# Two placements in an attention and SwiGLU kernel: PSUM tile and copy engine of batch 1's first transposes, and the gap of the second-softmax value product

## The chip, the cores and the metric

One core of a Trainium2 chip runs the whole program. The metric is device time in microseconds (us), lower is better; a time is the median of several executions. Before: 369.15 us (368.29 to 369.44, three runs), and 369.29 us with a fourth run (369.80), the value that the changed kernel is compared with.

Engines: PE multiplies matrices, VectorE (DVE) and ScalarE (ACT) do elementwise work, GpSimd (POOL) issues the casting and gathering transfers and a few masks, SP issues plain and transposing transfers. PEld in the profile is PE's weight load, which overlaps its matmuls here: PE is busy for 350.1 us and PEld for 175.2 us of a span of 366.2.

## The reference, cut to what matters

```python
# q, k, v: (8 batches, 8 heads, 576 positions, 64); 8 global positions
mask = |i - j| <= 32  or  i is global  or  j is global
attn = softmax(where(mask, q @ k.T / 8, -1e9))
x    = (attn @ v) laid out as (8 * 576 tokens, 512)
out  = (silu(x @ w_gate) * (x @ w_val)) @ w_out        # 512 -> 1536 -> 512
```

## The kernel before

The feed-forward part runs in nine chunks of 512 tokens, each of twelve gate units and four output units. After each unit comes a gap into which pieces of the attention of later batches are put by hand, in the order in which they are written. A piece that wasn't ready held up what follows it in the profile of before: PE sat idle 2.52 us ahead of the first transposes of batch 1, and the next gate, which needs nothing of them, started behind them at 35.27 us.

The score matmuls of this kernel read q and k with the head dimension on partitions (64 of them: `ps_s<-qT,kT 64*128 64x64` in the profile). Batches 0 to 2 transpose on PE (step T). The global keys' and queries' scores come from gathered rows that POOL masks into a tile kqm, transposed on PE (step GT). The "second softmax" is that of the global queries over all keys: its weights p are transposed into p2t (step P2T; by PE up to batch 3, by a DMA transpose on SP for batches 4 to 7) and multiplied with v (step AV2, line 462). The result becomes gvt on DVE, which each later value product (step AV, line 546) reads first.

```python
psc = tile_pool(bufs=1, space=PSUM)   # score pair, tag "sc"
pm  = tile_pool(bufs=1, space=PSUM)   # tile m
pf  = tile_pool(bufs=4, space=PSUM)   # gates and outputs

def step_T(hp):                       # one head pair of batch 1 or 2
    pool, tag = (pm, "m") if (hp in (0, 2) if b == 1 else hp == 3) else (psc, "sc")
    pair = pool.tile([P, 2, 1024], BF16, tag=tag, name="ps_t")
    # ... 12 transposes of k, 12 of q
    nc.scalar.copy(out=kT[...], in_=pss[0])
    (nc.scalar.copy if hp % 2 else nc.vector.tensor_copy)(out=qTs[b][...], in_=pss[1])

def gate(fc):
    if t0 == 0 and fc == 2:
        pair = pm.tile([P, 2, CH], FP32, tag="m", name="pgv")   # gate 2 borrows tile m
    # ... 4 matmuls to pg, 4 to pv; then ACT: tanh; DVE: gv = (th + 1) * pg; h = gv * pv

def loads_b():                        # POOL, in this order
    load_qk_part(1, loaded[1], 0); load_qk_part(1, loaded[1], 1)
    load_wgv(2)
    g1 = gather(1)
    load_v(1, range(0, 3))
    kqms[1] = gather_mask(*g1)
    load_v(1, range(3, 5))
    # ... output weights

# casts of k and q of batch b to bf16 in DRAM (POOL), o = 16 * (b - 1):
    if b > 4: cast_at[b] = o - 32 + 8
```

The softmax here doesn't subtract the row's maximum and nothing guards it: scores larger than these inputs give would overflow.

Of the kernel before, what the change touches and what calls it, by code (L numbers as in the profile page):

```python
# [26 lines left out]
def kernel(  # L27
# [11 lines left out]
    nc = tc.nc  # L39
# [32 lines left out]
    psc = ctx.enter_context(tc.tile_pool(name="psc", bufs=1, space=bass.MemoryType.PSUM))  # L72
    pm = ctx.enter_context(tc.tile_pool(name="pm", bufs=1, space=bass.MemoryType.PSUM))
# [264 lines left out]
    def attention(b):  # L338
# [24 lines left out]
        def step_T(hp):  # L363
            if hp == 0:
                qTs[b] = bp.tile([P, HP, S], BF16, tag="qT", name="qT")
            pool, tag = (pm, "m") if (hp in (0, 2) if b == 1 else hp == 3) else (psc, "sc")
            pair = pool.tile([P, 2, 1024], BF16, tag=tag, name="ps_t")
            pss = []
            for n, name in enumerate(("k", "q")):
                ps = pair[:, n, 0:S].rearrange("p (j i) -> p j i", j=LJ)  # L370
                pss.append(ps)
                src = loaded[b][name]
                for j in range(LJ):
                    for par in range(2):
                        nc.tensor.transpose(  # L375
                            out=ps[64 * par : 64 * par + 64, j, :],
                            in_=src[:, 2 * hp + par, D * j : D * (j + 1)],
                            identity=ident[0:LP, 0:LP],
                        )
            nc.scalar.copy(  # L380
                out=kT[:, hp, WIN : WIN + S].rearrange("p (i j) -> p i j", j=LJ),
                in_=pss[0].rearrange("p j i -> p i j"),
            )
            (nc.scalar.copy if hp % 2 else nc.vector.tensor_copy)(
                out=qTs[b][:, hp, :].rearrange("p (i j) -> p i j", j=LJ),
                in_=pss[1].rearrange("p j i -> p i j"),
            )
# [256 lines left out]
        L = lambda f, *a: (lambda: f(*a))  # L644
# [31 lines left out]
        if b < XQ:  # L676
            return [
                [L(step_T, 0)], [L(step_T, 1)],
                *([[L(step_T, 2)], [L(step_GT), L(step_T, 3), vb]] if b == 1 else
                  [[L(step_GT), L(step_T, 2)], [L(step_T, 3), vb]]),  # L680
            ] + mid + end
# [2 lines left out]
            [L(step_S2), L(step_SG)],  # L684
            [L(step_S, 0), L(step_P2T)],
            [],
            [L(step_S, 1)],
            [L(step_S, 2), L(step_AV2)],
            [L(step_S, 3), L(step_AV, 0), L(step_X, 0)],
            [L(step_AV, 1), L(step_X, 1)],  # L690
            [L(step_S, 4), L(step_AV, 2), L(step_X, 2)],
# [91 lines left out]


    head, xa2, xa3, s4, av8, x8 = attention(0)
    for f in head:
        f()
# [32 lines left out]
    for b, o in ((1, 2), (2, 15)):  # L820
        for i, g in enumerate(attention(b)):
            gaps[o + i] = gaps.get(o + i, []) + g
    for b in range(XQ, B):
        steps = attention(b)
        o = 16 * (b - 1)
        for i, g in enumerate(steps):
            slot = o + 1 + (16 * i) // len(steps)
            gaps[slot] = gaps.get(slot, []) + g
        if b > XQ:
            tr_at[b] = o - 16 + 5  # L830
        if b > 4:
            cast_at[b] = o - 32 + 8
        v_at[b] = o - 16 + 2
        g_at[b] = o - 16 + 6
        m_at[b] = o - 16 + 13
# [43 lines left out]
```

## Time and profile before

| before | value | read as |
|---|---|---|
| median | 369.15 us | 368.29 to 369.44 |
| profiled execution | 367.98 us, span 366.2 us | the profile of one execution |
| PE busy | 350.1 us, 96% | the bound |
| DVE, ACT, POOL busy | 64%, 42%, 27% | off the path except where PE waits for them |
| granted TensorE clock | 1.000 in the profiled execution | 9 in all 40 slices of the row PEclk |

A line of the waits view reads: who waited, for whom, then total us, number of waits and the longest. A line of the timeline reads: start, duration, engine, line, operation, out<-in, shape, count, and in brackets the idle time before it and what ended it.

### The profile page before, as it was taken

How to read it: one execution, taken by the hardware profiler on the slowest of the kernel's cores; microseconds unless marked ns; L12 is line 12 of the kernel's file. 1: busy time of each engine (PE TensorE's matmuls, PEld its weight loads, DVE VectorE, ACT ScalarE, POOL GpSimd, SP SyncE). 2: the span in 40 equal slices, each digit the busy share in tenths (PEclk: the TensorE clock that was granted, in tenths of full speed). 3: DMA queues.
4: the chain of work that ended last, by engine and by line, in shares of the span. 5: the costliest groups of instructions: out<-in, count | busy, mean ns of one | idle time of the engine just before them, and what ended most of it. 6: DMA issues, size and time to landing. Idle time of an engine off the chain costs nothing.

```text
span 366.2 us, 7993 instructions
## 1 busy us (share of the span) xinstructions
PE 350.1 (96%) x3290; PEld 175.2 (48%) x3290; DVE 235.3 (64%) x469; ACT 152.8 (42%) x237; POOL 97.5 (27%) x114
## 2 busy tenths in 40 slices
PE   2887999999999999999999999999999999999996
PEld 1564545554544454444444454444544454444444
DVE  6665787268944885588548854886488728824850
ACT  4734573467323552355225532552354323323322
POOL 7925455934444001450246013100000000000000
PEclk9999999999999999999999999999999999999999
DMA  7999999999999926999999999941340131011002
GB/s 103 142 209 204 120 188 200 167 214 138 140 160 199 191 55 111 138 141 150 147 141 139 157 131 145 175 69 54 107 100 2 43 113 27 0 57 60 0 9 109
DMA packets 141638, 43.52 MB, mean 119 GB/s; under 512 B 126369, under 2 KB 135841, under 8 KB 141601
## 3 DMA queue, kind: packets, MB, share of 16 engines
q0 software_dynamic: 93824, 19.40, 64.4%
q1 hardware_dynamic: 47776, 23.60, 31.2%
q8 instruction: 26, 0.43, 0.5%
q14 instruction: 12, 0.09, 0.1%
HBM read 38.28 MB, written 15.34 MB: 146 GB/s over the span
## 4 chain that ended last, share of the span: by engine, by line
PE 80%; DMA 10%; POOL 4%; DVE 3%; ACT 2%; issue 1%; POOLq 0%; DVEq 0%
PE po L772 25%; PE pg L711 23%; PE pv L711 22%; DMA kg<-in_k_dram,gofs 4%; DMA wg_sb<-in_moe_w_gate_dram 3%; PE ps_av L546 3%; PE ps_s L493 2%; DMA vb<-va 2%; PE ps_av L555 2%; ACT pe L501 1%; POOL va L102 1%; DMA va<-in_v_dram 1%; DVE pt L507 1%; DVE gvt L469 1%; PE po L759 1%; PE ps_t L375 1%
## 5 line engine op out<-in xcount | busy, mean ns | idle before, releaser
L711 PE MATMUL pg<-xT,wg_sb 128*128 128x512 bf16 x420 | 108.3, 380 | 0.0
L711 PE MATMUL pv<-xT,wv_sb 128*128 128x512 bf16 x420 | 107.8, 379 | 0.0
L744 DVE SCALAR_TENSOR_TENSOR gv<-th,pg 128x512 bf16<-128x512 bf16 x107 | 73.3, 685 | 39.7 <-ACT th L742 39.0
L742 ACT ACTIVATE th<-pg 128x512 bf16<-128x512 f32 x107 | 63.9, 598 | 80.5 <-PE pg L711 76.7
L772 PE MATMUL po<-wo_sb,h 128*128 128x512 bf16 x420 | 94.5, 379 | 0.0
L748 DVE TENSOR_TENSOR h<-gv,pv 128x512 bf16<-128x512 bf16 x107 | 73.6, 688 | 11.5 <-PE pg L711 0.5
L711 PEld LDWEIGHTS <-wv_sb 128*128 128x128 bf16 x424 | 41.5, 98 | 50.0
L772 PEld LDWEIGHTS <-h 128*128 128x128 bf16 x420 | 39.9, 98 | 46.3
L102 POOL DMA_DIRECT2D va<-in_v_dram x40 | 35.2, 989 | 96.9 <-PE ps_av L555 73.5
L711 PEld LDWEIGHTS <-wg_sb 128*128 128x128 bf16 x424 | 37.0, 98 | 40.9 <-issue 1.7
L777 ACT ACTIVATE osb<-po 128x512 f32<-128x512 f32 x35 | 20.9, 597 | 81.7 <-PE po L772 79.7
L501 ACT ACTIVATE pe<-ps_s 128x1024 bf16<-128x1024 f32 (+1 forms) x40 | 37.5, 938 | 17.3 <-PE ps_s L493 16.6
L507 DVE TENSOR_TENSOR pt<-pe,band 128x1024 bf16<-128x1024 bf16 (+1 forms) x40 | 25.4, 636 | 20.3 <-ACT pe L501 20.3
L522 DVE TENSOR_REDUCE den<-ps_av 128x8 f32<-128x16 f32 (+1 forms) x40 | 6.7, 168 | 35.9 <-PE ps_av L555 33.6
L528 DVE TENSOR_TENSOR xa<-ps_av,den 128x512 bf16<-128x512 f32 (+1 forms) x40 | 25.5, 638 | 1.6 <-DMA xT<-xa 0.2
L546 PE MATMUL ps_av<-gvt,pg 128*64 128x264 bf16 x128 | 18.1, 295 | 1.0 <-DVE gvt L477 1.0
L493 PEld LDWEIGHTS <-kT 64*128 64x128 bf16 x576 | 11.3, 98 | 16.0 <-issue 15.0
L555 PE MATMUL ps_av<-va,pt 128*64 128x66 bf16 x256 | 18.0, 198 | 0.0
L555 PEld LDWEIGHTS <-pt 128*64 128x64 bf16 x512 | 17.6, 114 | 0.8 <-DMA vb<-va 0.7
L555 PE MATMUL ps_av<-vb,pt 128*64 128x66 bf16 x256 | 17.7, 198 | 0.3 <-DMA vb<-va 0.2
L493 PE MATMUL ps_s<-qT,kT 64*128 64x64 bf16 x576 | 16.2, 196 | 1.1 <-ACT pe L501 1.1
L109 POOL DMA_DIRECT2D qf<-in_q_dram x5 | 14.0, 2806 | 0.0
(122 smaller groups left out, 220.7 us busy)
## 6 DMA issues: line engine op xcount, KB each, us to landing
out_dram<-osb SPq DMA_DIRECT2D x35, 256.0 KB, 2.1
vb<-va SPq DMA_DIRECT2D x14, 264.0 KB, 5.6
va<-in_v_dram POOLq DMA_DIRECT2D x24, 128.0 KB
kf<-in_k_dram POOLq DMA_DIRECT2D x5, 576.0 KB
qf<-in_q_dram POOLq DMA_DIRECT2D x5, 576.0 KB
k_bf<-in_k_dram POOLq DMA_DIRECT2D x6, 288.0 KB
q_bf<-in_q_dram POOLq DMA_DIRECT2D x6, 288.0 KB
va<-in_v_dram POOLq DMA_DIRECT2D x16, 96.0 KB
```

What stands on the lines that cost most here:

```text
L102: nc.gpsimd.dma_start(out=va[lo:hi, u, :, 0:D], in_=vs[t0 + lo : t0 + hi])
L493: nc.tensor.matmul(out=ps[:, par, 64 * slot : 64 * slot + 64], lhsT=kT[r : r + 64, hp, 64 * t : 64 * t + P], rhs=qTs[b][r : r + 64, hp, 64 ...
L501: nc.scalar.activation(out=pe, in_=ps[:, :, 0 : 64 * ns].rearrange("p r (s c) -> p r s c", c=64), func=AF.Exp, scale=SCALE,)
L507: mult = lambda: nc.vector.tensor_tensor(out=pt.rearrange("p r s c -> p (r s) c"), in0=pe.rearrange("p r s c -> p (r s) c"), in1=bc(band, ...
L528: nc.vector.tensor_tensor(out=xa.rearrange("p (g h) d -> p g h d", g=g), in0=bc(ps, pst + [[1, D]]), in1=bc(den, [[4, g], [1, 4], [0, D]]) ...
L546: nc.tensor.matmul(out=ps[64 * e : 64 * e + 64, hg], lhsT=st["pg"][:, P * tp + 64 * e : P * tp + 64 * e + 64], rhs=st["gv"].rearrange("p h ...
L555: nc.tensor.matmul(out=ps[64 * e : 64 * e + 64, hg, hl, :], lhsT=pt[:, hl % 2, 4 * (hl // 2) + 2 * (tp % 2) + e, :], rhs=(va if e == 0 els ...
L711: nc.tensor.matmul(out=ps[:, 0:n], lhsT=w[:, cc, P * fc : P * (fc + 1)], rhs=xT[:, cc, t0 : t0 + n], start=(cc == 0), stop=(cc == NCC - 1),)
L742: nc.scalar.activation(out=th[:, 0:n], in_=pg[:, 0:n], func=AF.Tanh, scale=0.5)
L744: nc.vector.scalar_tensor_tensor(out=gv[:, 0:n], in0=th[:, 0:n], scalar=1.0, in1=pg[:, 0:n], op0=ALU.add, op1=ALU.mult,)
L748: nc.vector.tensor_tensor(out=st["h"][:, fc, 0:n], in0=gv[:, 0:n], in1=pv[:, 0:n], op=ALU.mult)
L772: nc.tensor.matmul(out=po, lhsT=st["h"][:, fc, P * ts : P * (ts + 1)], rhs=wo_sb[:, fc, :], start=(fc == 0), stop=(fc == NFC - 1),)
```

## The change

The intent: gate 2 fills tile m, and the first transposes of batch 1, next on PE, want the same tile; they wait until DVE has read it, 2.52 us in the profile of before. In the score pair they need not wait. That pair is needed again by the next head pair, so both copies go to ScalarE. Second, the value product of the second softmax is put behind the second score group in place of the third, so that gvt is ready when the first value product asks for it.

```diff
-            pool, tag = (pm, "m") if (hp in (0, 2) if b == 1 else hp == 3) else (psc, "sc")
+            pool, tag = (pm, "m") if hp == (2 if b == 1 else 3) else (psc, "sc")
@@
-            (nc.scalar.copy if hp % 2 else nc.vector.tensor_copy)(
+            (nc.scalar.copy if hp % 2 or (b == 1 and hp == 0) else nc.vector.tensor_copy)(
@@   steps of batches 3 to 7
-            [L(step_S, 1)],
-            [L(step_S, 2), L(step_AV2)],
+            [L(step_S, 1), L(step_AV2)],
+            [L(step_S, 2)],
```

"Part one" below is the first two edits, "part two" the third.

## The prediction

> **What bounds the kernel now.** I read the busy shares first, then the waits of PE, then the timeline around each wait that the change aims at, and last the landing times of the transfers that the moved work reads.
>
> ```profile
> span 366.2 us, 7993 instructions
> PE 350.1 (96%) x3290; PEld 175.2 (48%) x3290; DVE 235.3 (64%) x469; ACT 152.8 (42%) x237; POOL 97.5 (27%) x114
> ```
>
> PE is the bound: it is idle for 366.2 - 350.1 = 16.1 us in all, so only what shortens or lengthens PE's idle time, or adds PE work, can move the end. The change adds no PE instruction. The waits of PE are therefore the whole account:
>
> ```profile
> PE ps_t L355 <- DMA k_bf<-in_k_dram: 6.4, 2, 6.1
> PE ps_t L375 <- DVE h L748: 2.5, 1, 2.5
> ...
> PE ps_av L546 <- DVE gvt L477: 1.0, 5, 0.2
> ...
> PE ps_av L555 <- DMA vb<-va: 0.2, 1, 0.2
> ```
>
> The second line is what part one removes, the third is what part two removes: 2.5 + 1.0 = 3.5 us, 0.9% of the span, if nothing takes their place. Columns are total, times, longest. The last line, 0.2 us for the shifted values vb, looks like nothing; it matters below.
>
> [...] the first transposes of batch 1 sit idle 2.52 us for the gate values, and the next gate, which needs nothing of them, starts after them at 35.27 us. [...] the transposed second softmax p2t lands 9.8 us after issue while casts of k and q issued on POOL are under way, 2.7 us when none is. [...] the same p2t issue is recorded as 2.24 us, against 9.8 us to landing.
>
> **Part one: first transposes of batch 1.** Before, the transposes of head pair 0 use the PSUM tile m that gate 2 has just filled, and wait until DVE has read it.
>
> ```profile
> 34.64 0.45 PE L375 MATMUL ps_t<-ident,k_bf 96*64 96x96 bf16 x12 [2.52 <-DVE h L748]
> 34.89 0.45 PE L375 MATMUL ps_t<-ident,q_bf 96*64 96x96 bf16 x12
> 35.27 1.04 PE L711 MATMUL pg<-xT,wg_sb 128*128 128x512 bf16 x4
> ```
> ```profile
> 33.50 0.91 POOL L102 DMA_DIRECT2D va<-in_v_dram  x1 [0.61 <-DMA q_bf<-in_q_dram]
> ...
> 41.65 0.40 POOL L247 TENSOR_TENSOR kqm<-kg,mka 128x128 bf16<-128x128 f32 x1 [5.80 <-DMA kg<-in_k_dram,gofs]
> 42.01 0.39 POOL L247 TENSOR_TENSOR kqm<-qg,mka 128x128 bf16<-128x128 f32 x1
> ```
>
> In the score pair the k transposes can start at 32.05 us, where the first weight load already stood. They take 34.89 - 34.64 = 0.25 us. The q transposes then wait for q_bf: the last increment of its semaphore is at 33.22 us in the trace's records. They take 35.27 - 34.89 = 0.38, so gate 3 starts near 33.22 + 0.04 + 0.38 = 33.64, not 35.27: 1.6 us sooner. That is the local gain, the rest of the 2.5 is already lost to q_bf.
>
> It does not last. Three gates later PE transposes kqm. It came there at 42.29, so it will come at 42.29 - 1.6 = 40.7; but POOL makes kqm only when the gathered keys land (41.51 by the records), at 41.65 + 0.40 = 42.05 and 42.01 + 0.39 = 42.40. POOL and that gather do not wait for PE. The second kqm transpose was at 42.46 before and will be there again: the 1.6 us turns into a wait on POOL of about 1.6. If it slipped through, the vb transfer would catch it: it lands at 55.48 by the records, and the first product with vb starts at 55.52 already. The DMA that feeds it (keys, values, vb) hangs on no PE work here.
>
> Moving the q copy adds one ACT copy (0.65 us, as the odd head pairs show) and removes one DVE copy (0.76). The next transposes also use the score pair and need both copies done: the k copy ends near 33.4, the q copy runs from about 33.75 to 34.4, and the next transposes come at 33.64 + (37.37 - 35.27) = 35.7. No wait, 1.3 us to spare. Part one is worth **0.0 us**.
>
> **Part two: second-softmax product one gap sooner, batches 3 to 7.** The order of instructions shows that the 20 matmuls of L462 move from behind the third score group to behind the second, two gates sooner; their DVE multiplies follow. Removed: five waits of 0.2 us of the first value product on gvt, 1.0 us. Batch 5 before:
>
> ```profile
> 203.28 0.41 PE L493 MATMUL ps_s<-qT,kT 64*128 64x64 bf16 x16
> 203.62 1.04 PE L711 MATMUL pg<-xT,wg_sb 128*128 128x512 bf16 x4
> ...
> 207.18 0.41 PE L493 MATMUL ps_s<-qT,kT 64*128 64x64 bf16 x16
> 207.52 0.47 PE L462 MATMUL ps_av<-va,p2t 128*32 128x132 bf16 x20
> ...
> 210.35 0.30 PE L546 MATMUL ps_av<-gvt,pg 128*64 128x264 bf16 x2 [0.19 <-DVE gvt L477]
> ```
> ```profile
> 195.29 2.24 SPq L448 DMA_TRANSPOSE p2t<-p  x1
> ```
> ```profile
> DMA to landing us min/median/max: 9.8/9.8/9.8
> ```
>
> The product used to be asked for at 207.52; it will be asked for at 203.62, the end of the second score group. Its p2t is issued at 195.29 and lands 9.8 us later (the last line is the landing view of p2t in this stretch): 195.29 + 9.8 = 205.1. **Two gates of slack were hiding a late transfer.** New wait in batch 5: 205.08 + 0.04 - 203.62 = 1.5 us (0.04 as for vb above).
>
> The same for the others, with the landing from the semaphore records: batch 4, asked for at 166.06, landed 167.03: wait 1.0 us. Batch 6, asked at 241.19, landed 232.81 + 2.7 = 235.5: none. Batch 7, asked at 278.75, landed 270.38 + 3.4 = 273.8: none. Batch 3 transposes on PE, and its copy ends at 124.31, asked for at 128.49: none. Batches 4 and 5 are late because the casts of k and q for later batches are issued at 154.91 and 192.46, just ahead of their p2t; for 6 and 7 there is no cast left. These starts are all paced by PE, so a shift of PE by some tenths moves both sides and leaves the waits.
>
> Nothing else grows: m is free when the product comes (its last reader, the exponential of the global scores, ended long before), and the 1.07 us of DVE multiplies move to a gap followed by one without attention work.
>
> **Sum.** Part one 0.0; part two -1.0 + 1.0 + 1.5 = +1.5 us. After batch 5 PE has no wait left in which to win it back, and all later work is PE's. From the median 369.15 I take **370.4 us**: 0.2 below the full sum[...].
>
> **Rivals.** (A) Both waits vanish and nothing replaces them: 369.15 - 3.5 = 365.7. For it speaks the list of waits; against it the kqm multiply and vb, both within 0.3 us of binding already. (B) p2t lands in time in batches 4 and 5, as in 6 and 7: -1.0, so 368.1. For it: [...] I have one trace; against: two batches of two with casts are late, by 1.0 and 1.5, and landings would have to improve by about a tenth each. (C) Part one lives in part, where gather and vb land sooner than in this trace: at most 1.6 less, so 368.8 with the waits of part two. (D) The two copies on ACT delay the next transposes in the shared score pair: at most some tenths, in front of the same kqm wait, so it costs nothing at the end. I give my own account about 70%, B 13%, C 12%, A 5%.
>
> **Range and chances.** The runs of before spread 1.15 us. Rival B gives the low side, landings half a microsecond later each the high side: 368.5 to 371.9. A gain of 2% would be 7.4 us, twice what all touched waits hold; a loss of 2% would need p2t five times as late. Faster 0.01, same 0.98, slower 0.01.
>
> **What would show it.** In the profile after: no wait of L375 on h; a short one of the q transposes on q_bf; a wait of L393 on kqm of more than 1 us, and the second kqm transpose still near 42.5; no wait of L546 on gvt; two waits of L462 on the DMA of p2t of about 1.0 and 1.5 us, in batches 4 and 5 alone. Wrong would be: the kqm transposes more than half a microsecond sooner (the gather moved with PE), or L462 without waits (B).

0.0 for part one and -1.0 + 1.0 + 1.5 for part two came to +1.5 us, 370.65 on the median of 369.15. That the forecast lies some 0.2 us lower, at 370.4, was the author's guess.

## The result, and the profile after

The changed kernel took **367.88 us** (367.72 to 368.09, four runs) against 369.29 us: ratio 0.9965, 95% interval 0.9943 to 0.9987. That is 0.35% faster, "same" at the 2% mark, and below the predicted range of 368.5 to 371.9.

The page of the changed kernel, span and busy line:

```profile
span 366.2 us, 7940 instructions
PE 345.8 (94%) x3236; PEld 175.2 (48%) x3290; DVE 235.5 (64%) x468; ACT 153.2 (42%) x238; POOL 96.6 (26%) x114
```

PE seems less busy, but 54 of its 3290 matmul records are missing here (the weight loads are complete), so this share can't be compared. The span is the same as before to 0.1 us, although the medians differ by 1.4: the two profiled executions, 367.98 and 367.97 us, were equally fast. So the profiles side by side can't show the gain; the difference must lie in what executions of before mostly do and its first profile did not.

The longest waits of PE in the changed kernel, after the 6.9 us on k_bf at the start:

```profile
PE ps_av L462 <- DMA p2t<-p: 2.0, 2, 1.3
PE ps_av L555 <- DMA vb<-va: 1.5, 1, 1.5
PE ps_s L493 <- ACT pe L501: 1.1, 1, 1.1
PE ps_av L462 <- DMA va<-in_v_dram: 0.6, 2, 0.4
```

The 2.5 us on h and the 1.0 us on gvt are gone. In place of the latter are two waits on p2t, as predicted. The waits on vb and va belong to batch 0, whose work the change doesn't touch; there this execution lost about 2 us that the first profile of before had not lost. The timeline of the changed kernel:

```profile
34.11 0.45 PE L375 MATMUL ps_t<-ident,k_bf 96*64 96x96 bf16 x12
34.39 0.42 PE L375 MATMUL ps_t<-ident,q_bf 96*64 96x96 bf16 x12
34.74 1.04 PE L711 MATMUL pg<-xT,wg_sb 128*128 128x512 bf16 x4
...
41.76 0.28 PE L393 MATMUL ps_g<-ident,kqm 128*128 128x128 bf16 x2
...
164.61 0.41 PE L493 MATMUL ps_s<-qT,kT 64*128 64x64 bf16 x16
166.34 0.36 PE L462 MATMUL ps_av<-va,p2t 128*32 128x132 bf16 x12 [1.32 <-DMA p2t<-p]
...
203.31 0.41 PE L493 MATMUL ps_s<-qT,kT 64*128 64x64 bf16 x16
204.39 0.41 PE L462 MATMUL ps_av<-va,p2t 128*32 128x132 bf16 x16 [0.68 <-DMA p2t<-p]
```
```profile
41.03 0.39 POOL L247 TENSOR_TENSOR kqm<-qg,mka 128x128 bf16<-128x128 f32 x1
```

The two lines of L462 are cut by the end of the stretch asked for; the product has 20 matmuls. Three readings. The transposes start without a wait. kqm was ready at 41.03 + 0.39 = 41.42 us, not at 42.40 as in the first profile of before, and PE, late from batch 0, came after it: no wait there. And p2t was late in batches 4 and 5, by 1.32 and 0.68 us.

### The profile page after: what moved, and what is told of

The parts are those of the page before. It is cut to its first block, busy times and chain, and to the rows that moved or that the text cites. A ratio compares the mean times of both kernels' runs of the same rounds, so it can differ in the third digit from the quotient of the medians.

```text
span 366.2 us, 7940 instructions
## 1 busy us (share of the span) xinstructions
PE 345.8 (94%) x3236; PEld 175.2 (48%) x3290; DVE 235.5 (64%) x468; ACT 153.2 (42%) x238; POOL 96.6 (26%) x114
## 4 chain that ended last, share of the span: by engine, by line
PE 85%; DMA 9%; POOL 2%; issue 1%; ACT 1%; DVE 0%; POOLq 0%; DVEq 0%
PE po L772 25%; PE pg L711 24%; PE pv L711 22%; DMA p2t<-p 5%; PE ps_s L493 3%; PE ps_av L546 3%; DMA vb<-va 2%; PE ps_av L555 2%; DMA va<-in_v_dram 2%; PE ps_t L375 1%; POOL va L102 1%; PE ps_av L462 1%; PE ps_s L427 1%; PE po L759 1%; PE ps_x L604 1%
## 5 line engine op out<-in xcount | busy, mean ns | idle before, releaser
L711 PE MATMUL pg<-xT,wg_sb 128*128 128x512 bf16 x390 | 105.9, 380 | 1.9 <-issue 0.3
L772 PE MATMUL po<-wo_sb,h 128*128 128x512 bf16 x404 | 92.4, 379 | 0.6 <-issue 0.2
```

The lines of the kernel that those rows point to most:

```text
L711: nc.tensor.matmul(out=ps[:, 0:n], lhsT=w[:, cc, P * fc : P * (fc + 1)], rhs=xT[:, cc, t0 : t0 + n], start=(cc == 0), stop=(cc == NCC - 1),)
L772: nc.tensor.matmul(out=po, lhsT=st["h"][:, fc, P * ts : P * (ts + 1)], rhs=wo_sb[:, fc, :], start=(fc == 0), stop=(fc == NFC - 1),)
```

## The experiments

Sixteen runs were made, in four sets of four, each set on one chip with its own runs of before (e3, e4, e13 and e14 repeat earlier kernels). Each run also has the mean granted clock of each timed execution, and that turned out to be the key. Three theories went in. **H**: the first profile of before had an unusually early batch 0 on PE. **P**: p2t is in time in most executions. **C**, formed after the first set: the 2.5 us of PE idle is often followed by a stretch of half clock.

### e1 and e2: the parts alone; e3 and e4: both kernels profiled again

Edits: the first two hunks of the change (e1), the third (e2), none (e3, e4).

> Part one alone (transposes of head pair 0 of batch 1 in the score pair, both copies on ScalarE). The prediction on record: 0.0 us, the wait for the gate values turns into a wait of L393 on kqm. Theory H (head): in the profile of after, batch 0 ran about 2 us later on PE than in the profile of before, because its vb and va landed later, so that kqm and vb of batch 1 no longer bound and the whole 2.5 us was kept; if most executions have such a late head, part one alone gains 2.0 to 2.5 us. Theory P (the waits on p2t seen in the profile of after are short in other executions): part one gains under 0.5 us.

> Part two alone (second-softmax value product one gap sooner in batches 3 to 7). Prediction on record: loses 1.5 us; the profile of after showed waits on p2t of 2.0 us against 1.0 us saved, so theory H expects a loss of 0.7 to 1.5 us, with two waits of L462 on p2t in batches 4 and 5. Theory P expects a gain of 0.5 to 1.4 us.

> The kernel before once more, for a second profile of its head. Theory H: the first value product of batch 0 that needs vb starts later than the 23.65 us of the first profile (towards 25.5), the wait of L375 on h is still 2.5 us and there is no wait of L393 on kqm; span about 1.5 us longer than 366.2. If the head is as in the first profile, span about 366.2 and theory H falls.

> The changed kernel once more, for a second profile. Theory H: either a late head again (batch 0 waits 1 to 2 us on vb or va, no wait of L393 on kqm) or an early head with a wait of L393 on kqm; in both, waits of L462 on p2t of 1.5 to 2.5 us in batches 4 and 5. Span 366.0 to 366.4. Theory P: waits on p2t under 0.5 us in all.

| on one chip | median us | ratio to before, 95% interval |
|---|---|---|
| before | 369.78 | |
| e1, part one | 366.78 | 0.9919 (0.9884 to 0.9954) |
| e2, part two | 369.66 | 0.9995 (0.9959 to 1.0032) |
| e3, before again | 369.58 (one run) | |
| e4, changed again | 367.39 (one run) | |

Part one is worth 0.81% here, 3.0 us, more than the whole wait of 2.5 us that it removes. Part two alone is neutral in time, though its profile has two waits on p2t of 3.0 us in all: theory P falls for the profiled executions. Theory H falls too: in e3 batch 0 was early, yet the span was 367.8 us. The reason stands in the clock row of e3's page:

```profile
PEclk9999899999999999999999999999999999999999
```

In the first profile the row is all nines. Three stretches of time by engine in e3, then the first two of them in the first profile of before (columns: stretch, its us, busy us and instructions of PE, PEld, DVE, ACT, POOL, then granted clock, DMA share, GB/s):

```profile
33.00:36.40 3.40, 1.44 (x28) 0.97 (x28) 1.90 (x5) 0.71 (x2) 1.69 (x2) 1.00 1.25 206
36.40:39.80 3.40, 3.40 (x40) 1.84 (x37) 2.68 (x6) 0.60 (x1) 0.00 (x0) 0.50 1.60 197
39.80:43.20 3.40, 3.40 (x44) 1.84 (x39) 1.47 (x3) 2.67 (x5) 1.99 (x4) 1.00 0.93 65
```
```profile
33.00:36.40 3.40, 1.76 (x30) 1.10 (x30) 1.90 (x4) 0.69 (x2) 1.79 (x2) 1.00 1.26 203
36.40:39.80 3.40, 3.40 (x48) 1.85 (x46) 2.46 (x6) 2.22 (x4) 0.00 (x0) 1.00 1.53 199
```

For 3.41 us behind the wait on h, PE ran at half clock in e3. It shows in the matmuls too:

```profile
34.96 0.45 PE L375 MATMUL ps_t<-ident,k_bf 96*64 96x96 bf16 x12 [2.52 <-DVE h L748]
...
36.51 1.91 PE L711 MATMUL pv<-xT,wv_sb 128*128 128x512 bf16 x4
```

The same four matmuls take 1.03 us at full clock. From these figures the estimate: a stretch of 3.41 us at half clock costs 3.41 x 0.5 = 1.7 us, and lowers the mean clock of a 367 us execution by 1.7 / 367 = 0.005, to the 0.995 that many executions of before show. On this chip 8 of its 11 executions have a mean clock of 0.995 or less (mean time 370.5 us) and 3 have not (368.0); of part one 1 of 8 has it. "Half clock in" below counts such executions; a mean doesn't say where in the execution the stretch lay.

The kept profiles show more. In all seven with a half-clock stretch before the last 10 us (e1, e2, e3, e6, e8, e11, e16; mean clock 0.994 or 0.995 in each), it begins a whole number of 3.41 us stretches after the point from which the trace records the full clock (in e3 13.65 us after, four stretches; in e1 20.48, six). In the first profile of before this point is at 22.74 us, in the changed kernel's at 23.99, and the full clock recorded from there lasts 344.75 and 341.33 us, 101.0 and 100.0 such stretches. Below, these stretches, counted on from that point in each profile, are called the grid. In the grid's stretch that holds most of the wait on h, PE worked 1.45 us in e3 (33.00 to 36.41), 0.89 in e2, 1.09 in e11 and 1.41 in e16, and the clock was halved in the next stretch; it worked 1.76 us in the first profile of before (32.98 to 36.40) and 1.86 in e15, and the clock stayed full. In e8 the grid split the wait, 2.46 and 1.85 us of work in the two stretches, and the clock stayed full behind it; its half-clock stretch begins earlier, at 25.41 us, behind a wait of batch 0 on vb of 1.5 us. So of the five profiles with the whole wait of 2.5 us three show half clock behind it.

And the profile of e4, the other way in which the change can go, with batch 0 early:

```profile
32.69 0.42 PE L375 MATMUL ps_t<-ident,q_bf 96*64 96x96 bf16 x12
33.04 1.04 PE L711 MATMUL pg<-xT,wg_sb 128*128 128x512 bf16 x4
...
41.03 0.59 PE L393 MATMUL ps_g<-ident,kqm 128*128 128x128 bf16 x2 [0.81 <-POOL kqm L247]
```

Here is the predicted wait on kqm, 0.81 us and 0.3 more between the two transposes (they start 0.36 us apart, against 0.06 in the changed kernel, where kqm was ready). But the gather landed sooner than in the first profile, so the second kqm transpose stood at 41.39 us and not at 42.46.

### e5: the idle time filled, the wait kept

```diff
-                [L(step_T, 0)], [L(step_T, 1)],
+                [*([L(warm, 10)] if b == 1 else []), L(step_T, 0)], [L(step_T, 1)],
```

`warm(10)` is ten dummy matmuls of 512 columns. Nothing that the first transposes wait for comes sooner.

> The kernel before with 10 dummy matmuls of 512 columns (2.2 us) in front of the first transposes of batch 1, inside the 2.5 us that PE idles there; nothing of the wait itself is removed. Theory C (clock): in the majority of executions of before this idle time is followed by one stretch of 3.41 us at half clock, which costs some 1.7 us; filled, the granted clock stays 1.0 and the times gather near the fast mode of before, 368.0 us, with a spread under 0.7 us: 1.0 to 1.8 us faster than the median of before. Theory L (the plain length of the wait is all that counts): same as before, 369.5 to 370 us, or slower, and the clock still drops.

Measured: 369.87 us against 370.75 of before on that chip, ratio 0.9985 (0.9944 to 1.0026). The clock stayed full in 5 of 6 executions, against 3 of 11 of before. So, as far as these counts go, the idle time has a part in setting the clock. But the times didn't gather near 368 as theory C expected: they spread from 368.07 to 372.69, and the interval includes no gain. The dummies also take one of the four tiles of the gates, a side effect that was not separated. In time this run is inconclusive: that filling the idle time wins time was not shown.

### e6: part two without batches 4 and 5

```diff
+            [L(step_S, 1), *([] if b in (4, 5) else [L(step_AV2)])],
+            [L(step_S, 2), *([L(step_AV2)] if b in (4, 5) else [])],
```

> Part one, and the product one gap sooner only in batches 3, 6 and 7, where p2t was never late. If the late p2t of batches 4 and 5 is what makes part two lose: 0.6 us (3 waits of 0.2) under part one alone, so near 366.2 us and 1.5 us under the changed kernel; no wait of L462 on p2t. If part two loses for another reason (more work of DVE in the earlier gap), it stays at or above part one alone, 366.8 us.

Measured: 367.88 us, ratio 0.9929 (0.9897 to 0.9961); no wait on p2t in the profile, as expected. Against e1's ratio of 0.9919 on another chip it shows no advantage. In 4 of its 6 executions the clock was halved, in the profiled one behind a wait at the kqm transposes of 1.3 us (the waits view puts it down to DVE, but the kqm multiply ended at 41.41 us and the first transpose started at 41.46): in this profile half clock followed a wait moved by part one too. The 0.6 us expected are not shown.

### e7: the changed kernel with the casts issued later

```diff
-            cast_at[b] = o - 32 + 8
+            cast_at[b] = o - 32 + 14
```

> The changed kernel whole, with the casts of k and q of later batches issued after the mask multiplies of POOL, so some 3 us later and behind p2t. If casts running beside p2t are what delays it: p2t lands within 4 to 5 us of its issue in batches 4 and 5, no wait of L462 on it, 366 us or less (the 2.0 us of waits of the changed kernel gone). If it is delayed by something else (the vb transfers ahead of it in the same queue alone), the waits stay near 1 and 1.3 us and the time near 367.5.

Measured: **366.33 us** against 370.75, ratio 0.9895 (0.9867 to 0.9923), by its ratio the best of all kernels here (366 us or less was expected). No wait on p2t is left. The landing view of p2t of batch 4 in e7, and the same view of the changed kernel:

```profile
DMA to landing us min/median/max: 3.9/3.9/3.9
```
```profile
DMA to landing us min/median/max: 9.6/9.6/9.6
```

In batch 5 the product follows its score group at once:

```profile
202.02 0.41 PE L493 MATMUL ps_s<-qT,kT 64*128 64x64 bf16 x16
202.36 0.47 PE L462 MATMUL ps_av<-va,p2t 128*32 128x132 bf16 x20
```

Moving the casts behind the mask multiplies of POOL (issued at 158.42 and 193.90 us in e7, 153.82 and 192.49 in the changed kernel) took the lateness away: the casts were its cause, as the prediction said. In batch 5 the first cast still went out 0.3 us before p2t (issued at 194.22), and p2t landed after 5.0 us, against 9.1 in the changed kernel.

### e8: only the copy moved

```diff
-            (nc.scalar.copy if hp % 2 else nc.vector.tensor_copy)(
+            (nc.scalar.copy if hp % 2 or (b == 1 and hp == 0) else nc.vector.tensor_copy)(
```

> The kernel before with only the copy of q of the first transposes moved to ScalarE, the PSUM tile unchanged. My account: nothing, the wait of L375 on h of 2.5 us stays, the clock drops as often as in before, 369 to 370 us. If moving the copy off VectorE has a share in the gain: over 0.5 us faster than before.

Measured: 370.54 us against 370.75, ratio 0.9995 (0.9967 to 1.0023), clock halved in 4 of 6 executions. No share of the copy shows (the interval reaches from -1.2 to +0.9 us), so the gain is put down to the PSUM tile; the tile moved without the copy was not run. In the profiled execution the half clock lay before the wait on h, so these counts hold stretches of other origin too.

### e9 to e12: the cap on kqm, and the late casts without part two

e9 is e7, e11 is before and e12 is part one, each with the gather of batch 1 issued first:

```diff
     def loads_b():
+        g1 = gather(1)
         loaded[1] = new_qk()
         load_qk_part(1, loaded[1], 0)
         load_qk_part(1, loaded[1], 1)
         load_wgv(2)
-        g1 = gather(1)
```

e10 is part one with the edit of e7.

> The changed kernel, casts late as in e7, and the gather of the global keys and queries of batch 1 issued ahead of its k, q and weight loads. If the gather is what caps part one in the head: no wait of L393 on kqm (1.7 us in e7), no half-clock stretch behind it, and a further gain of up to 1.7 us over e7 on the same chip, as far as vb of batch 1 lets it through: 1.2 to 1.5% faster than before. If vb binds: the same as e7, with a wait of L555 on vb of batch 1 of over 1 us.

> Part one and the late casts, without part two. If part two is worth its 1.0 us once p2t is in time: 1.0 us slower than e7 would be on this chip, five waits of L546 on gvt of 0.2 us, no others; so about as part one alone, 0.8% faster than before. If the late casts themselves were the gain of e7: as fast as e7, 1.05% faster than before.

> The kernel before with the early gather alone. The wait of L375 on h of 2.5 us stays and the clock drops as often (about 7 in 10); kqm is not waited for. Same as before within 0.7 us.

> Part one with the early gather, against e11. If kqm is what caps part one: faster than e11 by about 2.2 us in executions of full clock (the wait of 2.5 less the start of q at its landing), plus about 0.7 of 1.7 us for the clock, so 3 to 3.6 us in the medians, and no half-clock stretch at all. If something else caps it (vb of batch 1): 2.5 to 3 us, as part one alone against before.

| on one chip | median us | ratio to before, 95% interval | half clock in |
|---|---|---|---|
| before | 370.98 | | 7 of 11 |
| e9 | 366.95 | 0.9897 (0.9868 to 0.9926) | 0 of 6 |
| e10 | 367.47 | 0.9921 (0.9880 to 0.9961) | 0 of 6 |
| e11 | 372.12 | 1.0035 (1.0001 to 1.0070) | 4 of 6 |
| e12 | 368.24 | 0.9928 (0.9900 to 0.9957) | 0 of 6 |

With kqm out of the way (it was ready by 34.5 us in e9, 33.4 in e11 and e12, and batch 1 never waited for it), part one is worth 372.12 - 368.24 = 3.9 us. Among the executions at full clock alone it is 371.20 (two) - 368.25 (six) = 2.95 us, not less than the wait of 2.5: with the cap gone the whole wait seems to be kept, though on two executions of e11. The early gather itself cost time, which was not expected (e11 is 1.1 us slower than before in the medians, e9 1.0% faster and not 1.2 to 1.5%): in e9, e11 and e12 score matmuls of batch 0 waited 1.7, 1.8 and 3.0 us for ScalarE, against 1.1 in all profiles without it; why is open. It may have eaten what e9 should have won over e7; that was about 0.9 us, since of the 1.7 us that the expectation names only 0.9 is batch 1's wait and 0.8 batch 0's. e10 against e7, 0.9921 to 0.9895, puts part two with p2t in time at 0.26% of 371, 1.0 us, which is its sum of waits; but the intervals overlap and the chips differ.

### e13 to e16: both parts on one chip, and the length of the idle time

e13 is the changed kernel, e14 part one alone. e15 and e16 are e5 with 4 and with 2 dummy matmuls.

> The changed kernel with five rounds, beside part one alone on one chip (e14), since so far the two were timed well only on different chips. My account: part two costs on top of part one what its two waits on p2t exceed the 1.0 us saved, 0.7 to 1.5 us; no or rare half-clock stretch; 2 to 2.5 us faster than before on this chip. If part two costs nothing on top: the same as e14.

> Part one alone, beside e13. My account: 0.7 to 1.5 us faster than e13, 3 us faster than before; a half-clock stretch in at most a third of the executions (behind the wait on kqm of up to 2 us).

> As e5 with 4 dummy matmuls in place of 10: 0.9 us of the 2.5 us filled, 1.6 us of idle left, less than half of a stretch of 3.41 us. If the clock halves where PE is idle for more than half of such a stretch[...]: no half-clock stretch, and as fast as e5 would be. If any idle time of that order does it: half clock in over half of the executions, as in before.

> As e15 with 2 dummy matmuls: 2.1 us of idle left. If more than half of a stretch at a random phase is what counts: half clock in about 6 of 10 executions, against 7 of 10 for before and none for e15. If only the full 2.5 us does it: none.

| on one chip | median us | ratio to before, 95% interval | half clock in |
|---|---|---|---|
| before | 368.79 | | 4 of 11 |
| e13, the change | 368.55 | 0.9994 (0.9960 to 1.0027) | 0 of 6 |
| e14, part one | 368.19 | 0.9984 (0.9943 to 1.0024) | 0 of 6 |
| e15, 4 matmuls | 368.28 | 1.0011 (0.9963 to 1.0059) | 1 of 6 |
| e16, 2 matmuls | 369.86 | 1.0025 (0.9982 to 1.0067) | 3 of 6 |

On this chip the gain is hardly there: before had the half clock less often, and its full-clock executions, but for one at 372.05, lay at 368.13 to 368.79. e14 spread from 366.58 to 370.82 at full clock, so there are other sources of spread. The expectations of 2 to 2.5 us for e13, of 3 us for e14 and of no half clock at all for e15 missed. e13 minus e14 is 0.4 us in the medians, the right sign and a third of what its waits on p2t (2.1 us less the 1.0 saved) would make; it is within the noise. The counts of e15 and e16 are too small to tell either from before's 4 of 11.

The waits of e15 and of e16 on h, from their two profiles:

```profile
PE ps_t L375 <- DVE h L748: 1.7, 1, 1.7
```
```profile
PE ps_t L375 <- DVE h L748: 2.1, 1, 2.1
```

The share of half-clock executions over the length of the idle time, all chips together: 0.4 us (e5) 1 of 6, 1.7 us (e15) 1 of 6, 2.1 us (e16) 3 of 6, 2.5 us (before in the four sets) 27 of 44; e2, e3, e8 and e11, also 2.5 us, 14 of 21. All kernels with the transposes in the score pair: 5 of 55, four of them in e6. In the grid's stretch around the wait on h, 3.41 - 1.76 = 1.65 us of idle left the clock full (before) and 3.41 - 1.45 = 1.96 us did not (e3). If a bound lay between them, at half of the 3.41 us, which is assumption and not shown, then an idle time of 2.5 us at a random phase would halve the clock with an estimated share of 0.73: 0.27 of the time the stretch holds all of it, else a boundary cuts it, and in 63% of those cuts one part is longer than 1.7. The measured 27 of 44 is 0.61, but e8 shows that such counts hold stretches that other waits set off. The exact rule is not settled. In e1 and e6 the clock halved behind waits of 1.3 to 1.4 us at kqm, though PE worked 1.92 and 1.96 us in the grid's stretch, over half of it transposes: whether transposes count like other matmuls was not tested. And in batch 0, 1.74 us of work in a stretch was followed by half clock in e8, 1.73 us in the changed kernel was not.

## Why the prediction was wrong

The range missed, and the step that failed is **"Part one is worth 0.0 us."** In its place e1 measured a gain of 3.0 us (0.81%) on one chip, e12 against e11 3.9 us with the cap removed, and e14 0.6 us, within the noise, on another. Step by step:

- **The local gain.** Predicted 1.6 us, cut by q_bf. In the later profiles of the change q_bf was in time (no wait in the changed kernel nor in e4; gate 3 stood at 33.04 in e4). At that point e4 had 2.2 us and not 1.6.
- **The cap at kqm.** The mechanism was right, its position was one draw. The second kqm multiply starts at 42.01 us in the first profile of before, and between 40.8 and 42.0 in the others with the same order of loads. The wait then takes back 1.1 us of e4's 2.2, not all. In full-clock executions part one kept 1.1 us on one chip (368.0 to 366.9, 3 and 7 executions) and none that can be seen on another.
- **What was not in the sum at all: the clock.** The sentence "only what shortens or lengthens PE's idle time, or adds PE work, can move the end" is false: PE work can also take longer, as in e3's half-clock stretch behind the wait. If removing the 2.5 us of idle also removed a stretch of 1.7 us in about 6 of 10 executions, that is 1.0 us on average, an estimate from the counts (27 of 44 before, 5 of 55 with the transposes in the score pair). The first profile of before was one of the other 4, so its page could not show it, but its being faster than all timed runs could have warned me. That the idle time has a part in setting the clock rests on the profiles by the grid and on e5 (half clock in 1 of 6, before 8 of 11); that the clock costs 1.7 us, on e3's stretch and on the means of full and half-clock executions of before (2.5, 1.2, 2.1 and 1.6 us apart on the four chips). No run removed the half clock alone and won that time: in e5, which meant to, no gain can be seen.
- **Copies and score pair.** No cost predicted, none that shows (e8; the next transposes of the change start without a wait).
- **Part two.** Right in mechanism: p2t late in batches 4 and 5 alone, because of the casts (e7). Predicted 1.0 and 1.5 us, measured 1.32 and 0.68 in the changed kernel, 2.0 in place of 2.5 in the sum. Net +1.0 in place of +1.5 by the profiles. The timed runs show less: e13 over e14 0.4 us in the medians and 0.6 in the means, which they don't resolve, and e2's interval against before, -1.5 to +1.2 us, leaves the predicted +1.5 out. So the size of this term was off too.
- **The sum.** -1.0 for the clock, 0 to -1.1 for the kqm cap, +0.4 to +1.0 for part two give -1.7 to +0.0. Measured: -1.4 us in the first measurement, -0.2 on the fourth chip. For the first one the clock of the timed runs of before is not on record, so how much of the 1.4 is the clock stays open. Rival B came near the first number with a wrong reason: it let p2t arrive in time. It and my number were both built on one profile's draw. The range wasn't even the sum of its parts: its low end, 368.5, left out rival B at 368.1, and two landings half a microsecond later make 370.4 + 1.0 = 371.4, not 371.9.

What stays open: why some full-clock executions are 2 to 4 us longer than their neighbours; where exactly the clock halves; and why part one shows so little on the fourth chip.

## What to carry to other kernels

A wait of PE may cost more than its length: behind 2.5 us of idle in the profiles of e2, e3 and e11, 2.1 us in e16, and 1.4 and 1.3 us at the kqm transposes in e1 and e6, the clock was halved for 3.41 us here; in the first profile of before 2.5 us was not followed by it. So compare the granted clock of every timed run, not of the profiled one alone. Take two or three profiles of the same kernel before concluding that a later wait will swallow a gain, because the cap set by a transfer moved here: kqm by up to 0.6 us between profiles of one kernel (e1 and e14, on different chips), by 1.2 us (41.2 to 42.4 us) among the fifteen with the same order of loads. And before asking sooner for a DMA's result, look at its landing and at which transfers are under way beside it (p2t of batch 4 landed 9.6 us after its issue behind the casts, 3.9 us ahead of them): here the better fix was to issue the casts 1.4 to 4.6 us later, which with the change made the kernel 1.05% faster than before (e7).
